# Exponents of the second matrix's pieces in PSUM, and the small units' feed-forward in pairs, in a fused top-k attention and feed-forward kernel

## The chip, the cores and the metric

The kernel runs on one core of one Trainium2 chip, in one launch. The metric is the device time of the core in microseconds; the median of three runs counts. The profile is of one execution more, with a time of its own.

## What is computed

Inputs are q, k and v of shape (8, 8, 576, 64): eight batches, eight heads, 576 rows of 64; and two matrices, w_in (512 x 2048) and w_out (2048 x 512). The two matrices come as float64. Cut to what matters, the reference is:

```python
scores = scale * np.matmul(q, k.transpose(0, 1, 3, 2))
kth = np.partition(scores, -top_k, axis=-1)[..., -top_k:-top_k + 1]   # top_k = 32
scores = np.where(scores >= kth, scores, -1000000000.0)
attn = softmax(scores)
x = np.matmul(attn, v), the heads side by side: 4608 x 512
h = x @ w_in
out = (h - np.tanh(h)) @ w_out
```

## The kernel before

**Steps.** The attention goes in 144 steps. A step takes 128 query rows of a pair of heads (`hp`), 576 keys for each. `plan` lists the steps: batch by batch, query block by query block. A `Unit` is a set of token blocks that goes through the feed-forward together. Batch 0 begins with two *small* units of one block (128 tokens) each, steps 0 to 3 and 4 to 7; all later units have two blocks.

**One step on the engines.** `scores` (TensorE, L351, then ScalarE's copy L359); `search` (VectorE, L381 to L404), which finds the 32nd largest of each row; `threshold` and `mask` (GpSimd L418, L427, L440, L444, ScalarE L437); `expo` (ScalarE L460). In batch 0 (`pe`), z is turned by TensorE: `turn_pe`, L554, with ScalarE's copies L557; two banks `zt` take these transposes and the product with v. `values` (L582, L592, L596) multiplies with v and writes the tokens xT.

**Weights.** Each matrix, being float64, is brought in by 16 pieces of 128 x 512, 0 to 15 for w_in and 16 to 31 for w_out, and converted bit by bit in `convert`: VectorE cuts the exponent out (L192), ScalarE makes a float32's exponent of it (L195, tile e), VectorE and ScalarE make the mantissa (L197, L200), VectorE puts the sign to the exponent (L203, reads e, writes f), GpSimd multiplies (L206). For w_in, e is a PSUM tile; for w_out it is f itself, in SBUF. The table `many` says how many pieces fall to each step: two in steps 0 and 1, three in steps 2 to 9, four in step 10. So w_in is converted in steps 0 to 5, w_out in steps 6 to 10. These instructions stand between the rounds of `search` in VectorE's order (`between`).

**Banks.** `next_h` hands out two PSUM banks in turn: to exponents e, and to the accumulators of the feed-forward (hps, ops).

**Feed-forward.** When the last step of a unit has had its `values`, `ffn(u)` puts the unit's items on the list `work`. A small unit has eight items `ffn_h` (first matrix, L640, two blocks of 128 hidden values each, so that two items fill one bank; the second of the two has tanh, a copy and a subtraction behind it, L652 to L654) and eight items `ffn_small_o` (second matrix, L661, two of 16 blocks each). Each item carries the number of pieces that have to be converted before it. `deal` is called several times in a step and issues items from the head of the list, as many as a share worked out by `rate` allows.

**What sets the order.** The program is written under a manual schedule: every engine runs its instructions in the order in which they are issued in this code, and waits only for data and for buffers. Within a step `n` that order is: turn of step n-2, mask of n-1, search of n with the conversions, scores of n+1, threshold, expo of n-1, `deal`, `values` of n-2, `deal`.

A float32 matmul appears in the profile as two records with a weight load each; transposes appear as one.

Of the kernel before, what the change touches and what calls it, by code (L numbers as in the profile page):

```python
# [55 lines left out]
def kernel(  # L56
# [20 lines left out]
    CD = DM // P  # L77
    CF = DFF // P
# [4 lines left out]
    WJ = 4  # L83
# [29 lines left out]
    def h_bank(k, name):  # L113
        return h_ps.tile([P, 512], FP32, tag=f"h{k}", name=name)

    def next_h(name):
        bank[0] ^= 1
        return h_bank(bank[0], name)
# [39 lines left out]
    def flat(x):  # L158
        return x.rearrange("p n w -> p (n w)")
# [13 lines left out]
    def convert(piece, slot):  # L173


        j, i = piece // CD, piece % CD
        if j < WJ:
            src, dst = moe_w_in[i * P : (i + 1) * P, j * NW : (j + 1) * NW], w_in[j][:, i, :]
        else:
            r0 = ((j - WJ) * FJ + i) * P  # L180
            src, dst = moe_w_out[r0 : r0 + P, :], w_out[j - WJ][:, i, :]
        raw, shifted, _ = slot
        nc.sync.dma_start(flat(raw), src.bitcast(U32))
        nc.sync.dma_start(
            flat(shifted).bitcast(U8)[:, 0 : 8 * NW - 4], src.bitcast(U8)[:, 3 : 8 * NW - 1]
        )
        yield
        hi = raw[:, :, 1]
        f = thpool.tile([P, NW], FP32, tag="th", name="f")
        fu = f[:].bitcast(U32)  # L190

        nc.vector.tensor_scalar(fu, hi, 20, 0x7FF, ALU.logical_shift_right, ALU.bitwise_and)  # L192

        e = next_h("e")[:] if j < WJ else f[:]
        nc.scalar.activation(e.bitcast(I32), fu, AF.Relu, bias=e896[:], scale=2.0**23)  # L195

        nc.vector.tensor_scalar(  # L197
            dst.bitcast(U32), shifted[:, :, 0], 0x0FFFFFFF, None, ALU.bitwise_and
        )
        nc.scalar.activation(dst, dst.bitcast(U32), AF.Copy, bias=1.0, scale=2.0**-28)  # L200
        yield

        nc.vector.scalar_tensor_tensor(  # L203
            out=fu, in0=hi, scalar=0x80000000, in1=e.bitcast(U32), op0=ALU.bitwise_and, op1=ALU.bitwise_or
        )
        nc.gpsimd.tensor_tensor(dst, dst, f[:], ALU.mult)  # L206
        yield
# [9 lines left out]
    def half(t):  # L217
        return slice(t * D, (t + 1) * D)
# [289 lines left out]
    def tiles(x, nq):  # L508

        x = x[:, 0 : nq * 2 * S]  # L510
        return x.rearrange("p (a k i j) -> p a k i j", a=NG, k=KC, j=G)
# [52 lines left out]
    def in_order(x, nq):  # L564

        return x.rearrange("p (a i j) -> p i a j", a=NG, i=nq)

    def values(n):


        g = steps[n]
        nq, u = g.nq, g.unit
        et = tiles(ets.pop(n), nq)
        w = nq * P
        av = zt_ps.tile([P, 2, N], FP32, tag="zt", name="av")
        for i in range(2 if g.rem else 1):
            cols = half(i) if g.rem else slice(0, w)
            es = et[:, 2 * i : 2 * i + 2] if g.rem else et
            hp = g.hp + i
            for c in range(J + 1):  # L580
                for t in range(2):
                    nc.tensor.matmul(  # L582
                        av[half(t), 0, cols],
                        vb[g.b, hp][:, t, c, :] if c < J else vrs[hp][:, t, :],
                        es[:, :, (J + 1) * t + c if c < J else J].rearrange("p a i j -> p a (i j)"),
                        start=(c == 0),
                        stop=(c == J),
                    )
        if g.pe:
            rx = rxs.pop(n)  # L590
            for i in range(nq):
                nc.tensor.transpose(  # L592
                    in_order(av[:, 1, 0:w], nq)[:, i], rx[:, i].rearrange("p t d -> p (t d)"), ident[:]
                )
            xs = xs0
            nc.scalar.copy(xs[:, :, 0:w], av[:, :, 0:w])  # L596

        def put(dst, order, cols):
            if g.pe:
                nc.gpsimd.tensor_tensor(dst, order(xs[:, 0, cols]), order(xs[:, 1, cols]), ALU.mult)  # L600
            else:
                nc.scalar.copy(dst, order(av[:, 0, cols]))

        if g.rem:
            for i in range(2):
                put(xt(u)[:, g.hp + i, g.col : g.col + R], lambda x: x, half(i))
        else:
            dst = xt(u)[:, g.hp, g.col : g.col + w].rearrange("p (i a j) -> p i a j", a=NG, i=nq)
            put(dst, lambda x: in_order(x, nq), slice(0, w))
        if n in done:  # L610
            work.extend(ffn(u))

    def xt(u):
        if u.xT is None:
            p = xpool if u.tag == "xT" else xrpool
            u.xT = p.tile([P, CD, N], FP32, tag=u.tag, name=u.tag)
        return u.xT
# [36 lines left out]
    def ffn_o(u, i, part):  # L656
        if part == 0:
            cur[u] = next_h("ops")
        for f in range(2 * part, 2 * part + 2):
            o = f * u.n + i * P  # L660
            nc.tensor.matmul(  # L661
                cur[u][:],
                u.g[0][:, o // 512, o % 512 : o % 512 + P],
                w_out[f // FJ][:, f % FJ, :],
                start=(f == 0),
                stop=(f == CF - 1),
            )
        if part < CF // 2 - 1:
            return
        ot = thpool.tile([P, DM], FP32, tag="th", name="ot")  # L670
        nc.scalar.copy(ot[:], cur[u][:])
        for rows, dst in u.blocks[i]:
            nc.sync.dma_start(dst, ot[rows, :])
# [265 lines left out]
    def combine_next():  # L939

        called[0] += 1
        send_kept(4)
        if combined[0] < len(COMBINE):
            x, j = COMBINE[combined[0]]
            if now[0] < (17 if x == "T3" else 20 if x in ("T2", "T4") else 0):
                return
            combine(x, j)
            combined[0] += 1

    def ffn_small_o(u, part):  # L950

        ffn_o(u, 0, part)
        if u.combines:
            combine_next()
# [10 lines left out]
    def ffn(u):  # L965

        nh = CF * u.n // (2 * P)
        full = len(u.blocks) == 2
        if u.tail:
            nh = 0  # L970
            for item in range(2 * len(ORDER)):
                yield CD * WJ, u, lambda item=item: ffn_s(u, item)
        for item in range(nh):
            f = (item + 1) * CF // nh - 1
            yield CD * (f // FJ + 1), u, lambda item=item: (ffn_full if full else ffn_h)(u, item)
        if not full:
            for part in range(CF // 2):
                yield CD * (WJ + part // 2 + 1), None, lambda part=part: ffn_small_o(u, part)
            return
        for item in range(2 * len(ORDER)):  # L980
            yield 2 * WJ * CD, None, lambda item=item: ffn_p(u, item)
# [3 lines left out]
    steps, done, work = [], {}, []  # L985
# [45 lines left out]
    def run(exact):  # L1031
# [43 lines left out]
        def load_piece():  # L1075
            k = len(loaded)
            usable = [x for x in free if x[2] > k]
            if k < pieces and usable:
                slot = min(usable, key=lambda x: x[2])
                free.remove(slot)  # L1080
                piece = convert(k, slot)
                next(piece)
                loaded.append((piece, slot))
# [75 lines left out]
        credit, coming_back = 0.0, []  # L1159

        def deal(part):
            nonlocal credit
            credit += part * share
            while work and credit > 0 and work[0][0] <= usable:
                work.pop(0)[2]()
                credit -= 1
            credit = min(credit, 1.0)

        for n in range(-4, NS + LAG):
            pe = here(-2) and steps[n - 2].pe  # L1170
            def due():
                for m in (n - LAG, n - LAG + 1, n - LAG + 2):
                    if 0 <= m < NS and steps[m].last and steps[m].lag == n - m:
                        values(m)
# [23 lines left out]
            if pe:  # L1198
                spread(n - 2)
            deal(0.0 if pe else 0.4)  # L1200
            if n >= NEAR:
                due()
# [9 lines left out]
            if here(-1):  # L1212
                expo(n - 1)
            deal(0.8 if pe else 0.2)
            if pe and steps[n - 2].last:
                values(n - 2)
            deal(0.0 if pe else 0.2)
            if here(-2) and not pe and steps[n - 2].last:
                coming_back.append(spread_keys(n - 2))
# [52 lines left out]
```

## Time and profile before

| | |
|---|---|
| time, median of 3 runs | 1476.77 us (1475.81 to 1477.08) |
| profiled execution, its own time | 1476.01 us |
| its span | 1474.2 us, mean granted TensorE clock 0.973 |
| PE busy | 1365.6 us (93%) |
| VectorE (DVE) busy | 1321.5 us (90%) |
| ScalarE (ACT) busy | 1033.2 us (70%) |
| GpSimd (POOL) busy | 1090.2 us (74%) |
| L203, 16 pieces of w_in | 0.66 to 0.68 us each |
| L203, 16 pieces of w_out | 0.68 to 1.57 us each |
| step 11 begins | 154.0 us into the span |

PE is TensorE's matmuls, PEld its weight loads. A busy share is an average over stages with different limits: the start, in which weights are converted, the long middle, and the end, in which only feed-forward is left. The page cuts the span into 40 slices of 36.9 us, a digit for the busy tenths of each engine; PEclk is the granted TensorE clock in tenths. A view by stretches gives busy time and number of records of each engine in any part of the span. A line of the timeline has start, duration, engine, source line, operation, output<-input, shapes and the number of merged records; in brackets stands the idle time before it and what ended it.

### The profile page before, as it was taken

The numbers are of one execution on the slowest core, as the hardware profiler recorded it, in microseconds if no ns is written. First come the engines' busy times: TensorE is split into PE (matmuls) and PEld (weight loads), VectorE is DVE, ScalarE is ACT, GpSimd is POOL, SyncE is SP. The second block draws the span as 40 slices with busy tenths as digits, with TensorE's granted clock in tenths as the row PEclk, the third lists the DMA queues.
The fourth block names the chain that finished last, engine by engine and source line by source line (L and its number), as shares of the span: only waits on it lengthen the run. The fifth ranks groups of instructions, "written<-read, shape, count | busy, mean of one in ns | idle before, by whom it ended". The sixth has DMA issues, their size and how long they took to land.

```text
span 1474.2 us, 37773 instructions
## 1 busy us (share of the span) xinstructions
PE 1365.6 (93%) x13316; PEld 871.1 (59%) x13316; DVE 1321.5 (90%) x4968; ACT 1033.2 (70%) x1921; POOL 1090.2 (74%) x1581
## 2 busy tenths in 40 slices
PE   4667899889999898999999999999999999999998
PEld 2455565455565555656556666666565666656885
DVE  7999988899999999999999999999999999886411
ACT  4776677778787777777687777777777777664421
POOL 3777679968788686969696969696969697868211
PEclk9787999999999999999999999999999999999999
DMA  9955103676767676686767767777676667643320
GB/s 273 381 184 168 53 21 90 169 195 167 196 173 197 164 183 180 160 209 152 190 152 192 179 174 177 194 168 185 167 184 172 171 167 200 157 141 108 89 53 32
DMA packets 241255, 241.90 MB, mean 164 GB/s; under 512 B 177440, under 2 KB 186144, under 8 KB 233888
## 3 DMA queue, kind: packets, MB, share of 16 engines
q1 hardware_dynamic: 238688, 239.09, 60.7%
q8 instruction: 108, 1.77, 0.5%
q14 instruction: 91, 0.75, 0.2%
q10 hardware_dynamic: 2368, 0.30, 0.2%
HBM read 153.47 MB, written 85.85 MB: 162 GB/s over the span
## 4 chain that ended last, share of the span: by engine, by line
PE 46%; DVE 36%; POOL 9%; DMA 3%; ACT 3%; issue 2%; SPq 0%; DVEq 0%; ACTq 0%; POOLq 0%
PE hps L626 14%; PE hx L626 10%; PE hy L626 8%; DVE m L401 7%; PE av L582 5%; PE scps L351 5%; DVE top L393 5%; DVE rest L404 5%; DVE zx L518 5%; DVE ab L387 3%; POOL z L440 3%; DVE top L404 2%; DVE ab L382 2%; POOL g L654 2%; DVE scps L381 2%
## 5 line engine op out<-in xcount | busy, mean ns | idle before, releaser
L440 POOL TENSOR_TENSOR z<-sc,z 128x576 f32<-128x576 f32 x288 | 406.8, 1435 | 66.4 <-ACT z L437 66.0
L626 PE MATMUL hps<-xT,w_in 128*64 128x256 f32 x3584 | 412.2, 385 | 3.7 <-ACT g L653 3.7
L626 PEld LDWEIGHTS hps<-xT,w_in 128*64 128x64 f32 x3584 | 252.5, 138 | 157.1 <-issue 30.6
L486 ACT ACTIVATE z<-z,rd 128x576 f32<-128x576 f32 x252 | 181.2, 767 | 88.3 <-DVE rd L479 87.9
L460 ACT ACTIVATE z<-z,nb 128x576 f32<-128x576 f32 x288 | 221.9, 776 | 13.1 <-POOL z L440 13.0
L437 ACT ACTIVATE z<-sc,tb 128x576 f32<-128x576 f32 x288 | 208.3, 776 | 24.6 <-POOL tb L418 19.8
L654 POOL TENSOR_TENSOR g<-g,th 128x512 f32<-128x512 f32 x128 | 163.9, 1281 | 63.4 <-ACT g L653 61.9
L393 DVE MAX8 top<-ab 128x8 f32<-128x144 f32 x864 | 194.7, 296 | 0.0
L359 ACT COPY sc<-scps 128x1152 f32<-128x1152 f32 x144 | 161.0, 1118 | 44.7 <-PE scps L351 43.9
L351 PE MATMUL scps<-kT,qT 64*64 64x288 f32 x2016 | 154.6, 422 | 30.3 <-DVE top L389 27.1
L518 DVE STREAM_TRANSPOSE zx<-z 128x1152 f32<-128x1152 f32 x126 | 171.7, 1363 | 7.6 <-ACT z L486 5.1
L401 DVE MAX8 m<-rest 128x8 f32<-128x168 f32 x576 | 161.8, 323 | 0.0
L401 DVE MAX8 m<-top 128x8 f32<-128x144 f32 (+1 forms) x576 | 153.1, 308 | 0.0
L626 PE MATMUL hx<-w_out,g 128*64 128x256 f32 x1088 | 129.2, 385 | 2.5 <-POOL g L654 2.4
L626 PE MATMUL hy<-more,g 128*64 128x256 f32 x1088 | 125.4, 380 | 0.0
L351 PEld LDWEIGHTS scps<-kT,qT 64*64 64x64 f32 x2016 | 66.7, 133 | 97.6 <-issue 26.4
L418 POOL TENSOR_SCALAR tb<-m 128x1 f32<-128x1 f32 x288 | 85.9, 307 | 35.0 <-DVE m L401 34.6
L387 DVE TENSOR_TENSOR ab<-scps,sc 128x576 f32<-128x576 f32 x144 | 107.7, 748 | 0.0
L626 PEld LDWEIGHTS hx<-w_out,g 128*64 128x64 f32 x1088 | 76.2, 138 | 49.9 <-POOL g L654 5.7
L626 PEld LDWEIGHTS hy<-more,g 128*64 128x64 f32 x1088 | 76.7, 137 | 43.7 <-issue 6.7
L652 ACT ACTIVATE th<-hps 128x512 f32<-128x512 f32 x128 | 75.1, 587 | 38.7 <-PE hps L626 35.3
L444 POOL TENSOR_SCALAR bad<-top,tb 128x3 uint8<-128x3 f32 x288 | 96.6, 343 | 0.1
(215 smaller groups left out, 2464.7 us busy)
## 6 DMA issues: line engine op xcount, KB each, us to landing
there<-zx SPq DMA_DIRECT2D x56, 1152.0 KB, 4.8
spare<-there SPq DMA_DIRECT2D x224, 288.0 KB, 5.5
more<-kept_T SPq DMA_DIRECT2D x33, 512.0 KB, 4.2
there<-zx SPq DMA_DIRECT2D x14, 576.0 KB, 7.2
spare<-there SPq DMA_DIRECT2D x56, 144.0 KB, 3.2
out_dram<-ot SPq DMA_DIRECT2D x31, 256.0 KB, 3.0
vb<-in_v_dram SPq DMA_DIRECT2D x48, 128.0 KB, 5.0
kin<-in_k_dram SPq DMA_DIRECT2D x82, 72.0 KB, 4.4
```

Of the source, the lines that this page charges most:

```text
L351: nc.tensor.matmul(ps[i * R : i * R + w, t, s, 0:S2], qT[g.b, hp, g.part][half(t), o : o + w], kT[g.b, hp][half(t), ks], start=True, stop= ...
L359: nc.scalar.copy(sc[:], ps[:, :, :, 0:S2])
L387: nc.vector.tensor_tensor(low[:, :, :, 0:W2], thirds(near), thirds(far), ALU.min)
L393: nc.vector.max(top[:, t, o : o + 8], low[:, t, i, :])
L401: nc.vector.max(m[:, t, m8], seen[i][t])
L437: nc.scalar.activation(zv[:, t, :], scf[:, t, :], AF.Relu, bias=tb[:, t : t + 1], scale=-BIG)
L440: nc.gpsimd.tensor_tensor(zv[:, t, :], scf[:, t, :], zv[:, t, :], ALU.subtract)
L460: nc.scalar.activation(x["zv"][:, t, :], x["zv"][:, t, :], AF.Exp, bias=x["nb"][:, t : t + 1], scale=scale, accum_out=den[:, t : t + 1],)
L486: nc.scalar.activation(x, x, AF.Copy, scale=rds[n][:, g.i, t : t + 1])
L518: nc.vector.transpose(tiles(zx, g.nq)[:, :, :, g.i, :].rearrange("p c k j -> p k c j"), z[:].rearrange("p (k c j) -> p k c j", c=NG, j=G),)
L626: nc.tensor.matmul(acc[half(t)], lhs[:, half(t)], rhs, start=start, stop=stop, skip_group_check=True)
L654: nc.gpsimd.tensor_tensor(g, g, th[:], ALU.subtract)
```

## The change

Three things are altered.

1. In `convert`, e is a PSUM tile for all 32 pieces, so w_out's exponents too take a bank of `next_h`.
2. The items of the second matrix of a small unit may not start before all 32 pieces are converted (before: each as soon as its own pieces were). And a new function `add`, which takes the place of `work.extend`, puts the first-matrix items of the second small unit ahead of the waiting second-matrix items of the first.
3. As long as not all pieces are converted (up to and including step 10), `deal` issues items two at a time, so that both items of one bank come one after the other and no exponent takes a bank between them.

```diff
-        e = next_h("e")[:] if j < WJ else f[:]
+        e = next_h("e")[:]
         nc.scalar.activation(e.bitcast(I32), fu, AF.Relu, bias=e896[:], scale=2.0**23)
...
         if n in done:
-            work.extend(ffn(u))
-
-
+            add(list(ffn(u)))
+
+
+
+    def add(items):
+
+        waiting = [i for i, x in enumerate(work) if x[1] is None]
+        if len(waiting) == CF // 2 and len(items) == CF:
+            at = waiting[0]
+            work[at:at] = [x for x in items if x[1] is not None]
+            items = [x for x in items if x[1] is None]
+        work.extend(items)
...
         if not full:
             for part in range(CF // 2):
-                yield CD * (WJ + part // 2 + 1), None, lambda part=part: ffn_small_o(u, part)
+                yield 2 * WJ * CD, None, lambda part=part: ffn_small_o(u, part)
             return
...
             while work and credit > 0 and work[0][0] <= usable:
-                work.pop(0)[2]()
-                credit -= 1
+                for x in range(1 if usable == 2 * WJ * CD else 2):
+                    work.pop(0)[2]()
+                    credit -= 1
             credit = min(credit, 1.0)
```

In the built program, TensorE's order from step 6 on then reads as follows (pairs of first-matrix items, u0 and u1 for the first and second small unit; zt for the eight transposes that open a step, and after the change in brackets what stands there before it):

```
step 6:  zt, L351, pair 1 of u0, values, pair 2 of u0   [before: pair 1, values, half of pair 2]
step 7:  zt, L351, pair 3 of u0, values                 [rest of pair 2, half of pair 3, values]
step 8:  zt, L351, pair 4 of u0, values                 [rest of 3, half of 4, values, rest of 4]
step 9:  zt, L351, values, pair 1 of u1                 [ops of u0, values]
step 10: zt, L351, pair 2 of u1                         [ops of u0]
step 11: zt, L351, pair 3 of u1, values, half of pair 4 [ops of u0, values]
```

## Prediction

> **What bounds the kernel now.** I read the page first, its slices above all. VectorE stands at 9 from the third slice to the thirty-second, and the granted TensorE clock is low in slices 2 to 4 only, from about 37 to 148 us:
>
> ```profile
> DVE  7999988899999999999999999999999999886411
> PEclk9787999999999999999999999999999999999999
> ```
>
> The change touches only the start (pieces 16 to 31 of the matrices, the two small units), so I took that stretch step by step. A step begins with the L381 record of `search`; the stretches below run from one to the next, for steps 5 to 13. Columns: length, then busy time and records of PE, PEld, DVE, ACT and POOL, then the granted clock, DMA share, GB/s.
>
> ```profile
> 67.57:79.39 11.82, 6.62 (x39) 4.43 (x38) 11.79 (x42) 9.09 (x18) 9.47 (x14) 0.64 0.87 334
> 79.39:93.11 13.72, 9.99 (x74) 7.94 (x71) 13.69 (x42) 10.53 (x23) 10.35 (x14) 0.81 0.31 93
> 93.11:108.83 15.72, 11.21 (x86) 9.96 (x86) 13.72 (x43) 9.92 (x21) 10.96 (x14) 0.88 0.66 217
> 108.83:122.53 13.70, 10.03 (x70) 8.00 (x70) 13.67 (x42) 10.06 (x21) 11.35 (x14) 0.77 0.52 168
> 122.53:138.19 15.66, 11.13 (x62) 7.63 (x62) 13.69 (x42) 10.55 (x21) 12.22 (x15) 0.89 0.55 196
> 138.19:153.99 15.80, 10.61 (x30) 5.57 (x30) 14.34 (x45) 9.55 (x17) 11.88 (x14) 0.75 0.47 150
> 153.99:161.16 7.17, 6.75 (x30) 3.70 (x31) 7.13 (x33) 5.86 (x13) 5.92 (x10) 0.61 0.11 37
> 161.16:169.81 8.65, 8.41 (x48) 4.42 (x47) 7.16 (x33) 4.38 (x9) 3.47 (x8) 1.00 0.01 2
> 169.81:176.99 7.18, 7.18 (x62) 6.53 (x61) 7.15 (x32) 6.59 (x15) 5.71 (x10) 1.00 0.30 79
> ```
>
> Up to step 10 VectorE is the bound: it is busy all through step 5 (three pieces of w_in, exponents in PSUM, 11.82 us) and through steps 6 and 8 (three pieces of w_out, exponents in SBUF, 13.7), and in 7 and 9 all but 2 us. From step 12 on PE is full and VectorE waits for it, by way of ScalarE (waits from 154 to 290 us):
>
> ```profile
> DVE scps L381 <- ACT sc L359: 9.3, 7, 2.3
> ```
>
> The order on every engine is fixed, so a delay of PE at step 12 goes through to the end of the program.
>
> Why w_out steps are longer, from the records of L203 (ns min/median/max):
>
> ```profile
> L203 DVE SCALAR_TENSOR_TENSOR f<-w_out,e x10: 662/674/684, 17.4 to 78.8; 128x512 uint32<-128x512 uint32 x10
> L203 DVE SCALAR_TENSOR_TENSOR f<-spare,f x8: 678/1380/1565, 91.6 to 152.5; 128x512 uint32<-128x512 uint32 x8
> L203 DVE SCALAR_TENSOR_TENSOR f<-w_out,f x5: 764/1205/1551, 86.3 to 135.1; 128x512 uint32<-128x512 uint32 x5
> ```
>
> And why step 7 has 2 us more (timeline, from step 5's second L203 to step 7's first; start, duration, and in brackets the idle time before it and what ended it):
>
> ```profile
> 70.92 0.59 ACT L557 COPY et<-zt 128x512 f32<-128x512 f32 x1 [0.48 <-PE zt L554]
> ...
> 77.73 0.67 DVE L203 SCALAR_TENSOR_TENSOR f<-w_out,e 128x512 uint32<-128x512 uint32 x1
> ...
> 85.29 3.74 PE L640 MATMUL hps<-xT,w_in 128*128 128x128 f32 x32
> ...
> 88.95 1.09 PE L582 MATMUL av<-et,vb 128*64 128x128 f32 x14
> ...
> 95.14 3.40 PE L640 MATMUL hps<-xT,w_in 128*128 128x128 f32 x16
> ...
> 99.07 1.08 ACT L557 COPY et<-zt 128x512 f32<-128x512 f32 x2 [3.25 <-PE zt L554]
> 100.03 1.45 ACT L437 ACTIVATE z<-sc,tb 128x576 f32<-128x576 f32 x2
> ...
> 101.37 0.72 ACT L195 ACTIVATE f<-f,e 128x512 int32<-128x512 uint32 x1
> 102.12 0.72 DVE L203 SCALAR_TENSOR_TENSOR f<-spare,f 128x512 uint32<-128x512 uint32 x1 [1.97 <-ACT f L195]
> ```
>
> The reader is to see a chain: PE's feed-forward matmuls stand ahead of the transposes zt; ScalarE's queue then runs L557, L437, L195; VectorE's first L203 waits for L195. From L557 to L203 it takes 102.12 - 99.07 = 3.05 us. In step 5 L557 begins 3.35 us into the step and L203 at 6.96 without a wait; there is about 0.2 us of slack. Each later start of L557 is a stall of VectorE.
>
> **What the Trainium skill says.** "SBUF — State Buffer", Who interferes with whom: a VectorE instruction with two SBUF inputs and a GpSimd one that reads SBUF exclude each other for a whole instruction. The trace agrees: 0.67 us with e in PSUM, also beside GpSimd's L206, up to 1.57 with both in SBUF. "ScalarE: Activation LUTs", Step-by-step: what each stage is for: ScalarE writes PSUM faster than SBUF. L195 takes 692 ns against 712: 0.02 us. "TensorE: Matmul & The Clock Gate", Step-by-step: what each phase is for: only weight loads are pulled ahead, matmuls stay in program order. No matmul here passes a waiting one. Same page, What's actually happening: after an idle window of about 3.4 us the PE clock is halved, until a busy window. The trace agrees: idle from 92 us, 0.50 from 95, full again at about 98.2.
>
> **The change, part by part.**
>
> *Exponents in PSUM.* Sixteen L203 fall to 0.67 us; in steps 6 to 10 L203 has 3.55, 3.49, 3.53, 3.47 and 4.01 us (the first with 0.08 of the step before). With the L192 that wait less for GpSimd, a w_out step without stalls should look like step 5: 13.72 - 11.82 = 1.9 us saved in each of steps 6 to 9, and about 1.3 + 0.6 (a DMA wait that a later step no longer sees) in step 10. Sum 9.5 us, on VectorE's path.
>
> *The wait that this adds.* An exponent tile now takes a bank by `next_h`, which alternates between the two banks of the feed-forward. The built order shows it: the first matmul of each pair of items in steps 6, 7, 8 and 10 carries a wait on VectorE that it had not. Counting tiles: pieces 16, 17, 18 take banks 1, 0, 1, so the pair in step 6 takes 0 and must wait for the L203 of piece 17, the second of the step. Steps 7 and 8 give the same, the second L203; step 10 the third. PE reached this place 5.9 us into step 6 (85.29 - 79.39); the second L203 ends 77.73 + 0.67 - 67.57 = 10.83 us into a step. Queued behind the waiting matmul on PE are the step's values (20 records, about 1.6 us), L592 and the next step's zt; on ScalarE tanh and copy (about 1.1 us) ahead of L596 and L557; behind those L437, L195 and so VectorE's L203.
>
> *Price of one pair.* 32 records: 3.74 us at full clock (117 ns each), 32 x 213 = 6.8 at half (3.40/16). PE idles some 4 us before each, so the clock will be half, for 3.4 us (16 records) or more: 3.4 + 16 x 0.117 = 5.3. I take 5.6; bounds 3.74 and 6.8.
>
> *Step by step*, from the start of step 6 (before: steps end at 13.7, 29.4, 43.1, 58.8, 74.6):
> - Step 6: VectorE 11.8. The pair runs 10.9 to 16.5, values and L592 to 18.3. The pairing puts a whole second pair (before: half) ahead of step 7's zt: 3.75, to 22.05; its tanh and copy, then L557 at 23.2; first L203 at 26.25, 14.4 into the step instead of 7.0. From first L203 to step end 4.9 (74.53 to 79.39). Step 7 ends at 31.15: 19.3 us instead of 15.7.
> - Steps 8 and 9: from one first L203 to the next 3.9 (second L203's end) + 5.6 + 1.6 + 0.2 + 0.7 (zt) + 3.05 = 15.05. Step 8 15.05 instead of 13.7; step 9 15.05 instead of 15.66 (its own half pair ahead of zt is gone). End 61.25.
> - Step 10: the second unit's first pair now stands ahead of zt: 1.95 (to L592) + 0.15 + 5.3 + 1.15 + 3.05 = 11.6 to its first L203, before 6.6. From there 9.18 less 1.5: end at 80.55, before 74.6.
> - Then PE: the pair of step 10 waits for the third L203 (79.15) and ends at 84.8; zt of step 11 follows, before at 74.8 (154.17). Ten us late on the engine that bounds from step 12.
> - What follows: feed-forward done by there is 64 records of 117 ns (7.5 us) instead of 20 of about 0.45 (9.0): 1.3 more remains. A warm clock in step 11, which ran at 0.61, gives back about 2.2 (zt 1.97 to 1.04, L351 2.2 to 1.3, ops 4.0 to 3.6). Net +9.1.
>
> *The rest.* Second matrices after step 10, the first matrices of both units first: the same items; by step 17 both orders have issued the same. GpSimd's subtractions (1.27 each) move from steps 14 to 16 into 10 to 13, beside VectorE. The first unit's output DMA (256 KB, 3.0 us to landing) goes some three steps later on SP's queue; nobody reads it, and its buffer comes round late. Later on single items change sides of an L351 (1.8 us), both ways. Nothing for these, 1 us either way.
>
> Sum against the profiled execution (1476.01, span 1474.2): 1485.1. The median is 0.76 above it: 1486.
>
> **Rivals.**
> - *Slower as worked out*: 1486, 0.74. With the pairs at half clock throughout (five times about 1.2) 1492; about 1480 where some start warm.
> - *A warm clock*: pairs at 3.74, five times about 1.8 less: the stalls eat just what PSUM saves, 1477, 0.10. Against it: PE idles over 3.4 us ahead of each pair, and the clock fell after such idle times at 95.
> - *The wait is covered, faster*: PE has slack (6.6 of 11.8 busy in step 5). If the path from the second L203's end to the next L557 fitted into 11.82 + 3.55 - 10.83 = 4.5 us, only 9.5 would be saved and the stall of step 9 (1.9) besides, less 1 to 2 for step 7: about 1467, 0.14. It decides at a pair plus values of 3.5 us; they take 5.3 at best. For it: VectorE bounds this stretch and gets work off.
> - GpSimd as the bound: 9.5 of 11.8 in step 5, with a subtraction 10.8: near, within the first case.
>
> **How the numbers follow.** This kernel is told from no change by about 0.2%, 3 us. Slower 0.76 (the first case and a little of its kin), same 0.10, faster 0.14. The range takes in the first case nearly whole, and the warm one: 1475 to 1493.
>
> **What would show it.** L203 at 0.67 throughout: first part right. PE idle ahead of hps in steps 6, 7, 8 and 10, released by VectorE's L203; step 7 near 19 us; half clock in the pairs; zt of step 11 near 164. Wrong if the hps in step 6 begin by 6 us into it, or if VectorE's first L203 in steps 7 to 10 doesn't wait for L195; then about 1467.

## The result, and the profile after

Six runs of each kernel, taken in turn: after 1484.5 us (1483.8 to 1485.8), before 1475.7 (1473.5 to 1477.1); ratio 1.0062, 95% interval 1.0049 to 1.0075. The change costs 8.8 us, 0.6%. The profiled execution took 1484.42 us, with a span of 1482.2. Below, the added lines push `ffn_h` from L640 to L649 and `ffn_small_o` from L661 to L670.

The same two rows of slices as before: VectorE is lower in slices 3 to 5 than it was, the clock in slices 1, 3 and 5 (slice 1 lies ahead of everything that the change touches); behind the eighth slice one digit of VectorE near the end is all that differs in these two rows.

```profile
DVE  7987789899999999999999999999999999896411
PEclk7777899999999999999999999999999999999999
```

Steps 6 to 11, in the columns of the table of before (length, then PE, PEld, DVE, ACT, POOL, clock, DMA share, GB/s):

```profile
79.15:90.96 11.81, 5.89 (x24) 4.02 (x23) 11.78 (x42) 9.08 (x18) 9.46 (x14) 0.52 0.26 86
90.96:109.42 18.46, 12.76 (x104) 11.62 (x103) 11.86 (x43) 11.03 (x22) 11.90 (x16) 0.87 0.55 185
109.42:124.91 15.49, 10.36 (x72) 8.99 (x71) 11.85 (x43) 10.15 (x20) 10.47 (x15) 0.72 0.40 139
124.91:139.60 14.69, 10.07 (x87) 8.53 (x86) 11.87 (x43) 10.16 (x20) 10.55 (x15) 0.85 0.69 232
139.60:160.27 20.67, 11.15 (x59) 9.74 (x57) 13.28 (x44) 10.50 (x21) 12.01 (x16) 0.67 0.36 117
160.27:170.23 9.96, 9.96 (x76) 9.17 (x75) 7.24 (x33) 6.09 (x14) 5.33 (x9) 0.76 0.29 71
```

The reader is to see two things. VectorE's own work is down to 11.8 us in steps 6 to 9 (before 13.7), which is the gain. And the steps 7 to 10 are longer than that work by 6.6, 3.6, 2.8 and 7.4 us: VectorE waits. From the start of step 6 to the end of step 10 it is 81.1 us, before 74.6.

What it waits for stands in the answer for L203 (forms with ns, then idle time before it in us and times, then who waited for it):

```profile
L203 DVE SCALAR_TENSOR_TENSOR f<-w_out,e x15: 659/672/689, 17.1 to 137.9; 128x512 uint32<-128x512 uint32 x15
L203 DVE SCALAR_TENSOR_TENSOR f<-spare,e x12: 661/671/689, 39.7 to 159.4; 128x512 uint32<-128x512 uint32 x12
L203 DVE SCALAR_TENSOR_TENSOR f<-zx,e x5: 671/674/687, 43.1 to 155.0; 128x512 uint32<-128x512 uint32 x5
...
  ACT e L195: 20.1, 4
...
  PE hps L649: 23.1, 4
```

L203 takes 0.67 us throughout. But four times VectorE stood idle ahead of it for L195, 20.1 us in all, and four times PE stood idle for it ahead of hps, 23.1 us: each engine waits for the other, by turns. The timeline from step 6 to the end of step 7 shows one round, and the start of the next:

```profile
90.03 5.37 PE L649 MATMUL hps<-xT,w_in 128*128 128x128 f32 x32 [4.13 <-DVE f L203]
...
96.74 3.74 PE L649 MATMUL hps<-xT,w_in 128*128 128x128 f32 x32
...
100.31 1.04 PE L554 MATMUL zt<-ident,z 128*128 128x128 f32 x8
...
101.53 1.09 ACT L557 COPY et<-zt 128x512 f32<-128x512 f32 x2
...
104.57 0.69 DVE L203 SCALAR_TENSOR_TENSOR f<-spare,e 128x512 uint32<-128x512 uint32 x1 [6.57 <-ACT e L195]
...
108.48 6.34 PE L649 MATMUL hps<-xT,w_in 128*128 128x128 f32 x32 [5.70 <-DVE f L203]
```

The pair of items gets its bank from the second L203 of step 6 (89.30 + 0.67) and runs at reduced clock; the second pair follows ahead of zt; and from L557 to the L203 of step 7 it is 3.04 us, as before. The first L203 begins 13.6 us into step 7; before, it was 9.0 there, and 7.0 in a step without a stall. The longest round is that of step 10:

```profile
152.61 0.69 DVE L203 SCALAR_TENSOR_TENSOR f<-spare,e 128x512 uint32<-128x512 uint32 x1 [7.11 <-ACT e L195]
...
159.07 6.63 PE L649 MATMUL hps<-xT,w_in 128*128 128x128 f32 x32 [8.20 <-DVE f L203]
```

At step 13 the delay against before is 10.1 us, at step 16 it is 9.6. One late step (141) takes 12.2 us in the profile of before and 10.5 in that of after, so the spans differ by 8.0 only. Of the ten kernels below five have it at 12.1 and five at 10.5; why, no run shows.

### The profile page after: what moved, and what is told of

It reads as the page before. It is cut to its first block, busy times and chain, and to the rows that moved or that the text cites. A ratio compares the mean times of both kernels' runs of the same rounds, so it can differ in the third digit from the quotient of the medians.

```text
span 1482.2 us, 37774 instructions
## 1 busy us (share of the span) xinstructions
PE 1363.4 (92%) x13316; PEld 873.9 (59%) x13316; DVE 1313.2 (89%) x4968; ACT 1033.6 (70%) x1921; POOL 1087.9 (73%) x1581
## 4 chain that ended last, share of the span: by engine, by line
PE 41%; DVE 39%; POOL 8%; DMA 6%; ACT 3%; issue 2%; SPq 1%; DVEq 0%; ACTq 0%; POOLq 0%
PE hps L635 11%; PE hx L635 9%; PE hy L635 7%; DVE m L401 7%; DVE zx L518 5%; DVE top L393 5%; DVE rest L404 5%; PE av L582 5%; PE scps L351 4%; DVE ab L387 3%; PE hps L649 3%; POOL z L440 2%; DVE top L404 2%; DVE ab L382 2%; DVE scps L381 2%
## 5 line engine op out<-in xcount | busy, mean ns | idle before, releaser
L661 ACT ACTIVATE th<-hps 128x512 f32<-128x512 f32 x128 | 75.1, 587 | 59.5 <-PE hps L635 34.7
```

## The experiments

All were timed in turn with the kernel before. The table gives the median (5 to 22 runs), the ratio to before with its 95% interval, and, from one profiled execution of each kernel, the lengths of steps 6 to 10 with their sum. The runs of one_pair_psum and three were made where before took 1477.4; for these two the ratio is to be read.

| kernel | median us | ratio | 6 | 7 | 8 | 9 | 10 | sum |
|---|---|---|---|---|---|---|---|---|
| before | 1475.9 | 1 | 13.7 | 15.7 | 13.7 | 15.7 | 15.8 | 74.6 |
| after | 1484.5 | 1.0062 (1.0049 to 1.0075) | 11.8 | 18.5 | 15.5 | 14.7 | 20.7 | 81.1 |
| order_only | 1482.4 | 1.0040 (1.003 to 1.005) | 13.7 | 18.1 | 13.7 | 13.7 | 21.6 | 80.8 |
| own_bank | 1477.7 | 1.0011 (0.9999 to 1.0022) | 12.4 | 17.0 | 13.6 | 12.3 | 21.7 | 76.9 |
| kept_warm | 1477.2 | 1.0010 (1.0004 to 1.0017) | 11.8 | 16.9 | 13.0 | 13.1 | 19.8 | 74.7 |
| pairs_only | 1475.9 | 0.9998 (0.9989 to 1.0007) | 13.7 | 19.1 | 13.5 | 13.7 | 15.8 | 75.8 |
| no_pairs | 1480.7 | 1.0029 (1.0017 to 1.0041) | 13.7 | 15.8 | 13.7 | 15.5 | 20.1 | 78.8 |
| one_pair | 1472.6 | 0.9979 (0.997 to 0.9988) | 13.7 | 13.7 | 13.7 | 13.7 | 15.8 | 70.7 |
| one_pair_own_bank | 1468.0 | 0.9945 (0.9927 to 0.9963) | 12.4 | 13.6 | 12.3 | 12.4 | 17.0 | 67.6 |
| one_pair_psum | 1485.7 (before 1477.4) | 1.0054 (1.0041 to 1.0067) | 11.8 | 15.9 | 14.8 | 15.9 | 17.8 | 76.2 |
| three_own_bank | 1477.1 | 1.0007 (0.9999 to 1.0014) | 12.4 | 17.0 | 18.8 | 15.8 | 15.3 | 79.2 |
| three | 1471.6 (before 1477.4) | 0.9958 (0.9944 to 0.9971) | 13.7 | 13.7 | 15.4 | 13.7 | 15.9 | 72.4 |

**The order without the PSUM exponents (order_only).**

```diff
-        e = next_h("e")[:]
+        e = next_h("e")[:] if j < WJ else f[:]
```

> The change with its order and pairing kept, but w_out's exponents back in SBUF, as in the kernel before: so no exponent takes a feed-forward bank, and the feed-forward's matmuls need not wait for VectorE. Theory (the cost is the wait for the bank): no record of hps in steps 6 to 10 is ended by VectorE's L203; L203 is back at 1.2 to 1.5 us; steps 6, 8 and 9 take about 13.7 us, step 7 about 17 and step 10 about 20 (in both a whole pair stands ahead of the transposes zt); the time is about 1480, 4 us over before. Rival (the order and pairing are the whole cost, the bank nothing): as the changed kernel, 1484.5, or above it, since the exponents' gain is gone.

Measured: +6.5 us. Steps 6, 8 and 9 came out as expected, and so did the pairs: none of them waits for L203. But the order costs more than the 4 us expected. The wait of VectorE from 79 to 175 us (total, times, longest) and step 10 on the timeline:

```profile
DVE f L203 <- ACT f L195: 11.1, 2, 6.7
```

```profile
139.98 6.52 PE L649 MATMUL hps<-xT,w_in 128*128 128x128 f32 x32
...
150.56 0.73 DVE L203 SCALAR_TENSOR_TENSOR f<-spare,f 128x512 uint32<-128x512 uint32 x1 [6.72 <-ACT f L195]
```

Two stalls, in the two steps that have a whole pair ahead of zt. The pair in step 10 took 6.52 us, nearly half clock throughout, and VectorE lost 6.72. So the order alone is enough to make steps 7 and 10 long, 18.1 and 21.6 us; steps 8 and 9, which took 15.5 and 14.7 with the shared bank, are back at 13.7.

**Exponents in a bank that the feed-forward does not use (own_bank).** While w_out is converted, `next_h` gives bank 1 to the feed-forward; of its sixteen pieces ten have their exponent in bank 0, and six keep it in SBUF, so that there are never more than two exponents in a row for the one bank (the expectations say fifteen; sixteen it is).

```diff
+    converting = [False]
...
-        bank[0] ^= 1
+        bank[0] = 1 if converting[0] and name != "e" else bank[0] ^ 1
...
-        e = next_h("e")[:]
+        if j < WJ:
+            e = next_h("e")[:]
+        else:
+            e = h_bank(0, "e")[:] if piece - WJ * CD in (0, 2, 3, 5, 6, 8, 9, 11, 12, 14) else f[:]
...
+            converting[0] = WJ * CD <= usable < 2 * WJ * CD
```

> The change, with its order, but while w_out is converted the feed-forward keeps to one bank and the exponents of ten of the fifteen later pieces take the other; the exponents of the rest stay in SBUF, so that no exponent is written in the bank that a pair of items is to use next. Theory (the bank's wait costs, PSUM itself gains): no hps waits for L203; steps 6, 8 and 9 about 12.4 us, step 7 about 16, step 10 about 19; about 1475, 9 us under the changed kernel. Rival (the wait on PE is covered, and the time goes to the order or to the clock): within 3 us of the changed kernel, 1482 to 1487. Two items on one bank run one behind the other with their tanh between, which may cost up to 1 us a pair.

Measured: 1477.7, 6.7 us under the changed kernel though six of the exponents are back in SBUF. VectorE's two stalls left are those of order_only, in steps 7 and 10; no pair waits for L203. So with the same order, the shared bank turns a gain of 4.7 us (order_only to own_bank) into a loss of 2.1 (order_only to after). The intervals of own_bank and after lie far apart; those of order_only and after just overlap, so the size of the 2.1 is uncertain. The time is 2.7 us over the expected 1475, with steps 7, 8 and 10 longer than expected by 1.0, 1.2 and 2.7. Step 10, which is held by PE, takes 21.7 us as it does in order_only (21.6): shorter work of VectorE gains nothing there.

**The clock (kept_warm).**

```diff
+            if part == 0.8 and n in (6, 7, 8, 10) and not exact:
+                warm = zt_ps.tile([P, 512], FP32, tag="zt", name="warm")
+                for x in range({6: 18, 7: 40, 8: 40, 10: 60}[n]):
+                    nc.tensor.transpose(warm[:, x % 4 * P : (x % 4 + 1) * P], ident[:], ident[:])
```

> The changed kernel with idle work for PE: ahead of the pair of items in steps 6, 7, 8 and 10 it transposes the identity 18, 40, 40 and 60 times into a zt tile that nobody reads, so that PE isn't idle while it waits for the bank. Nothing else differs. Theory (the pairs run at half clock and stand on the path, so each microsecond of a pair is one of VectorE's stall): the clock stays full in steps 6 to 8 and at the end of 10, the four pairs behind the wait take 3.74 instead of 5.37, 6.34, 5.47 and 6.63, and steps 7, 8 and 9 are shorter by that; together 8.9, so about 1476. Rival (the pair's length is hidden, only the wait for L203 counts): time as the changed kernel, 1484. Second rival (the extra transposes overrun the wait): slower still.

Measured: 1477.2, 7.3 us less than the changed kernel by nothing but useless work. Step 6 on the timeline of PE (L1175 are the added transposes), then the pair of step 7:

```profile
85.78 2.13 PE L1175 MATMUL warm<-ident 128*128 128x128 f32 x18
90.16 3.84 PE L649 MATMUL hps<-xT,w_in 128*128 128x128 f32 x32 [2.25 <-DVE f L203]
```

```profile
107.11 3.84 PE L649 MATMUL hps<-xT,w_in 128*128 128x128 f32 x32 [1.24 <-DVE f L203]
```

The pairs of steps 6, 7 and 8 take 3.84 us instead of 5.37, 6.34 and 5.47, and steps 7, 8 and 9 are shorter by 1.52, 2.45 and 1.63: microsecond for microsecond. The fourth fell short, 5.46 instead of 6.63 where 3.74 was expected: the clock fell to half once more while it ran (the last section has the figures). So step 11 is shorter by 1.0 instead of 2.9; against that the first pair of step 10, which nothing was meant to warm, took 5.78 instead of 6.77, and step 10 is shorter by 0.85. The rival that calls the length of a pair hidden is out.

**The two halves of the order (pairs_only, no_pairs).** Each is the kernel before with one half: items dealt in pairs, or the first matrices of both units ahead of the second ones (`add`, and the second ones due only when all is converted).

```diff
-                work.pop(0)[2]()
-                credit -= 1
+                for x in range(1 if usable == 2 * WJ * CD else 2):
+                    work.pop(0)[2]()
+                    credit -= 1
```

> Of the change only the dealing in pairs, nothing else: exponents of w_out in SBUF, second matrices at once behind their unit's first ones. The order alone cost 6.5 us in the run before; this asks which half of it does. Theory (feed-forward ahead of zt costs VectorE its own length): step 7 has a whole pair ahead of its zt instead of half of one, about 18.1 instead of 15.7, and step 9 has none, 13.7 instead of 15.7; step 10 as before, 15.8. Net +0.4, time 1476 to 1477. Rival (the pairs are what costs, by their length at half clock): +4 or more.

Measured: no change. Step 7 is 3.4 longer and step 9 2.0 shorter; the 1.2 left at the end of step 10 has gone by step 13, since step 12 takes 7.1 instead of 8.65.

```diff
-            work.extend(ffn(u))
+            add(list(ffn(u)))
...
-                yield CD * (WJ + part // 2 + 1), None, lambda part=part: ffn_small_o(u, part)
+                yield 2 * WJ * CD, None, lambda part=part: ffn_small_o(u, part)
```

> Of the change only the new order of the two small units, the first matrices of both ahead of the second ones, and second ones not before all pieces are converted; items dealt one by one, exponents in SBUF as in the kernel before. Theory (the second unit's first pair now stands ahead of zt in step 10, at half clock): steps 6 to 9 as before, step 10 21.5 instead of 15.8; time about 1481 to 1482. Rival (the order costs later, on PE): step 10 near 16, the time still 1481.

Measured: +4.8, with step 10 at 20.1 and the steps ahead of it as before. Most of the order's 6.5 us is this one place: the second unit's first pair ahead of zt in step 10. It took 5.17 us here (from 138.50) and 6.52 in order_only, which may be most of the 1.7 us by which the two halves fall short of the whole.

**No feed-forward ahead of zt (one_pair), and then PSUM in a bank of its own (one_pair_own_bank).** From the kernel before; the second has the lines of own_bank besides.

```diff
         def deal(part):
             nonlocal credit
+            if usable < 2 * WJ * CD:
+                for x in range(0 if part < 0.8 or not work else 2 if work[0][1] else 5):
+                    assert work[0][0] <= usable
+                    work.pop(0)[2]()
+                return
```

> The kernel before, its exponents in SBUF, with one thing changed: while w_out is converted, feed-forward is issued only behind a step's second score block, one pair of items in each step from 6 to 9, and five items in step 10, none ahead of the next step's zt. Theory (feed-forward ahead of zt is what holds VectorE in steps 7 and 9, by ScalarE's queue): VectorE's first L203 of steps 7 and 9 waits for nothing, both steps take 13.7 instead of 15.7; about 1472, 4 us under before. Rival (VectorE's stall moves: the feed-forward left over is paid later on PE, which is the bound from step 12): the 4 us are gone again by step 13, time as before, 1476.

> The kernel before with one pair of feed-forward items a step and none ahead of zt, and besides ten of the fifteen later w_out pieces' exponents in a PSUM bank that the feed-forward does not use while w_out is converted. Theory (PSUM's gain is real where no wait comes with it): steps 6 to 9 about 12.4 us each, step 10 about 14.8; about 1466, 10 us under before and 18 under the changed kernel. Rival (the conversion is bound elsewhere too, by GpSimd at 9.5 to 12 us a step or by PE at half clock): steps near 13, about 1470. Second rival (what is won by step 11 is lost to feed-forward that is left over on PE): near 1475.

Measured: 1472.6 and 1468.0. In one_pair the stalls of steps 7 and 9 are gone, and 3.3 us of the 4 stay. With the bank of its own another 4.6 us come off. Steps 6, 7 and 10 of one_pair_own_bank:

```profile
79.63:92.02 12.39, 10.52 (x74) 8.08 (x71) 12.36 (x43) 9.64 (x20) 9.49 (x14) 0.74 0.25 89
92.02:105.57 13.55, 7.95 (x70) 6.61 (x70) 13.52 (x43) 9.70 (x18) 11.13 (x15) 1.00 0.65 226
...
130.27:147.23 16.96, 13.21 (x40) 6.18 (x38) 16.19 (x44) 11.65 (x23) 12.44 (x16) 0.90 0.47 155
```

VectorE is busy through step 7 (13.52 of 13.55), so what is left there is its own work, stretched, and no wait. Step 10 was expected at 14.8 and took 17.0: VectorE is busy for 16.19 of it (one_pair 14.49), with two of its instructions (L202 at 135.24, L194 at 136.79) at 1.6 us where others of their kind take 0.4, and 0.6 us go to waiting for a piece's DMA. This kernel beats before and after, at 0.9945 of before, 2 us short of the expected 1466.

**The same order, the bank shared (one_pair_psum).** one_pair with `e = next_h("e")[:]` for all pieces, as in the change. The order on PE is that of one_pair; against one_pair_own_bank the bank of the exponents differs, and the six that were in SBUF.

> The kernel with one pair of items a step, none ahead of zt (1472.6), with all exponents of w_out in PSUM as the change puts them: on the two banks that the feed-forward uses too. Against the kernel with the exponents in a bank of their own (1468.0) only the bank differs, and no feed-forward stands ahead of a zt in steps 6 to 9 in either. Theory (the wait for the bank alone costs): the pair in steps 6 to 8 waits for the second L203 of its step, the first L203 of the next step for the pair; step 6 takes 11.8, steps 7 to 9 about 14.5 to 15.5 instead of 12.4 to 13.6, step 10 about 17; the time is about 1475, 7 us over the one with a bank of its own. Rival (only feed-forward ahead of zt cost, the bank nothing): steps 7 to 9 at 11.8, about 1466.

Measured: 1.0054 against 0.9945, 1.1% or 16 us where 7 were expected. PE's waits (79 to 175 us), and the place that I had missed:

```profile
PE hps L640 <- DVE f L203: 19.5, 4, 5.1
```

```profile
154.82 2.07 PE L661 MATMUL ops<-w_out,g 128*128 128x512 f32 x2 [7.99 <-DVE f L203]
```

Steps 7 to 9 are 15.9, 14.8 and 15.9, the theory's 14.5 to 15.5 or a little over. But the second matrices take a bank by `next_h` too: in step 10 PE waits 8.0 us for L203, then runs 20 records of ops, and step 11 takes 13.2 us instead of 7.2. These 6 us are the bulk of the miss. In the change itself this cannot occur, since its second matrices come after the conversion. Of the 20.5 us between the two spans 15.7 are there by step 13. Step 141, long in this profile and short in the other, makes 1.6; some 3 come between steps 33 and 73, which have the same work in both, on another chip, and stay unexplained.

**Three items a step (three_own_bank, three).** `3` for `2` in the lines of one_pair, and an item is issued only where its pieces are converted.

> The fastest so far (one pair a step behind the second score block, ten exponents in a bank of their own, 1468.0) with three items instead of two in each of steps 6 to 9, and five at most in step 10, all of them still behind the second score block: feed-forward done in PE's slack ahead of step 11 is no longer owed in the stretch where PE is the bound. Theory (PE's idle time there is free as long as zt isn't late): steps 6 to 9 stay at 12.4 to 13.6, and about four items of 1.9 us less are left for later: 1460 to 1464. Rival (three items at half clock, on one bank one behind the other, make the next zt late): steps of 14 to 16, 1468 to 1474.

> The kernel with one pair of items a step (1472.6, exponents in SBUF), with three items in each of steps 6 to 9, on the two banks in turn; five at most in step 10. With three items and a single bank the second ones waited up to 6.3 us for ScalarE's copy (1477.1). Theory (an item that needs a bank whose copy is queued late on ScalarE holds PE and so zt; with two banks only the third item is in that place): a third hps still waits for the copy of the first, steps 7 and 8 at 15 to 17, time 1474 to 1477. Rival (PE's slack is free once there are two banks): steps 6 to 9 at 13.7, time 1466 to 1469.

Measured: 1477.1 and 1471.6. Both theory and rival of the first missed (the rival had the direction, with steps of 14 to 16; they took 17.0, 18.8 and 15.8): it lost all that one_pair_own_bank had won over before. With three items a step a second tile is opened on the only bank, and its first item waits till ScalarE has copied the tile ahead of it (L645 and L658 are here what L640 and L653 are in before):

```profile
109.72 6.67 PE L645 MATMUL hps<-xT,w_in 128*128 128x128 f32 x32 [6.25 <-ACT g L658]
```

That is once more a queue behind a wait, only the one who holds the bank is ScalarE. With two banks (three) no hps waits, and steps 6 and 7 are 13.7 long with 48 records instead of 32: PE's slack was free there, as the rival said. Step 8 is 15.4 with VectorE busy for 15.34 of it, so its own work was stretched, and 0.2 percentage points (0.9958 against 0.9979) are all that came out of it, with intervals that just touch.

The kernel before with the PSUM exponents and nothing else was not run, nor the change without its `add`: what they would take stays open.

## Why the prediction was right, point by point

- *Exponents in PSUM.* Confirmed on VectorE: its busy time in steps 6 to 9 fell from 13.7 to 11.8. As a saving of time it came about in full in step 6 alone (13.72 to 11.81); behind it VectorE waits anyway. Where no wait came with it, ten of sixteen exponents were worth 4.7 us (order_only to own_bank) and 4.6 (one_pair to one_pair_own_bank).
- *The wait that this adds.* As worked out: PE idle for L203 in steps 6, 7, 8 and 10; own_bank took it away and 6.7 us with it.
- *Price of one pair.* The term that was sized least well. Taken 5.6 (5.3 in step 10); measured 5.37, 6.34, 5.47, 6.77 and 6.63. The mean is 6.1, half a microsecond over: in three of five the clock stayed low for longer than the 16 records that I had taken from one place. Of the warm rival (1477, with five pairs at 3.74) kept_warm shows three pairs and parts of two others, and 1477.2. That the two figures meet is chance: with the two pairs of 5.78 and 5.46 at 3.74 too, it would be near 1473, an estimate from these lengths.
- *Step by step.* Steps 6 to 9: 11.8, 19.3, 15.05, 15.05 predicted; 11.81, 18.46, 15.49, 14.69 measured. Step 7 is shorter because its first pair took 5.37, and because with the clock full again there were 1.3 us from its end to the next pair, not 1.8. The end of step 10 came at 81.1 (80.55), zt of step 11 at 86.4 (84.8): 0.8 early at the end of step 9, then 1.5 and 1.0 late by the pairs of 6.77 and 6.63.
- *What follows.* From zt of step 11 to step 13 the delay fell from 11.4 to 10.1 us, by 1.25 where 0.9 was worked out. The net 9.1 then stands against 9.6 in the trace and 8.8 in the medians. The path was right; that the sum came so near owes something to luck, since its parts are off by up to 1.5 us and cancel.
- *Slips that cost little.* VectorE stands at 9 in slices 2 to 5 and 9 to 34 of before and at 8 in 6 to 8, not at 9 throughout; nothing rests on it. The feed-forward that remains is 9.0 - 7.5 = 1.5 us more, not 1.3. And the slack of L557 is nearer to 0.6 us than to 0.2: in step 7 of before it begins 2.6 us later than in step 5, and VectorE stalls for 1.97.
- *The rival "covered, faster", 1467.* Here the working was wrong, though the case did not come up. It left out that the order alone, without any wait for a bank, costs step 10 its 5.8 us: own_bank, with ten of the sixteen exponents in PSUM, shows 1477.7 for that case, and 1467 takes the order of one_pair besides (1468.0). The prediction's sum for steps 7 and 10 holds both causes, but it gave the order no price of its own; the runs show two of nearly the same size. Against before: order alone +6.5, and the exponents in PSUM on top of it +2.1, of which about -4.7 is the gain and +6.7 the bank.

## What to carry to other kernels

A PSUM tile taken in turn from a pool shares its wait with everybody on that pool: before moving an operand there, list who takes the next bank, when its last reader ends, and what is queued behind the taker on each engine. Where a stretch is bound by one engine, work of another goes behind the instructions that feed it; pairs of 5.2 to 6.5 us ahead of them, at the clock that they really got, cost VectorE 4.4 to 6.7 us here (order_only, pairs_only, no_pairs). And try the parts apart: together order and operand lost 0.6%, while the operand in a bank of its own, with no feed-forward ahead of zt, gained 0.55%.

## What the hardware showed beside that

- The same 32 records took 3.74 to 6.77 us. In step 6 of kept_warm PE was busy from 82.3 to 85.7 us, and the clock rose to full just as the transposes began; eighteen of them (2.13 us) ahead of a wait of 2.25 us kept it there, and the pair took 3.84. In step 10 sixty of them ahead of a wait of 1.86 us did not. Two stretches of each place, one after the other, in the columns of the table of steps:

```profile
85.80:89.10 3.30, 2.10 (x19) 1.86 (x18) 3.30 (x10) 2.83 (x6) 3.30 (x5) 1.00 0.41 78
89.20:92.50 3.30, 2.34 (x21) 2.34 (x22) 3.27 (x10) 2.86 (x7) 3.14 (x3) 1.00 0.96 331
...
150.60:154.00 3.40, 1.54 (x14) 1.30 (x12) 3.06 (x7) 2.39 (x5) 1.71 (x2) 1.00 0.13 53
154.10:157.40 3.30, 3.30 (x17) 3.30 (x17) 3.27 (x11) 1.51 (x4) 2.41 (x6) 0.50 0.42 120
```

  Here PE at work for 2.1 us in 3.3 was followed by full clock, and for 1.5 in 3.4 by half; where the limit lies no run shows. In the changed kernel the clock stood at half from 79.7 to 93.2 us, so the 5.37 us of its pair in step 6 are not due to the 4.13 us of idle time alone.
- Taking a stall away made VectorE's other work longer. In step 8 of kept_warm VectorE's first L192 and L197 fall beside GpSimd's subtraction, and its busy time is 12.9 us instead of 11.85 in the changed kernel. The group of L192 in that step, in kept_warm and then in the changed kernel (busy us, mean ns):

```profile
L192 DVE TENSOR_SCALAR f<-w_out 128x512 uint32<-128x512 uint32 x1 | 1.2, 1171 | 0.0
```

```profile
L192 DVE TENSOR_SCALAR f<-w_out 128x512 uint32<-128x512 uint32 x1 | 0.4, 415 | 0.0
```

The Trainium skill, "SBUF — State Buffer", Who interferes with whom, says that a `tensor_scalar` in a two-port mode takes the ports that VectorE shares with GpSimd, and that the one who comes second is blocked until the other's instruction has ended. The record agrees in time: this L192 began at 112.53, 0.39 us into a subtraction of 1.27, and ended 0.29 behind its end; that it runs in such a mode no trace shows. So the 11.8 us of a step with PSUM exponents are not a floor that holds in every order; in kept_warm VectorE was busy for 12.9 us in each of steps 7 to 9.
